# Two attention layers, chunk by chunk: a new order of the work, and the residual by way of DRAM

## The chip, the core and the metric

The kernel runs on one core of one Trainium2 chip. A core has a matrix engine (PE), a vector engine (DVE), an activation engine (ACT), a general-purpose engine (POOL) and a queue processor (SP) that here issues nearly all DMAs. Each engine carries out its own list of instructions strictly in the order in which it was written, and waits at an instruction until the semaphores that it needs are set. The metric is the device time of one execution in microseconds; the median of three executions is compared.

## What is computed

x is 2048 tokens by 512 numbers in float32. Four layers follow one another, A, B, A, B, each with a residual; both A layers share one set of weights and both B layers another.

```python
def _A_ref(x, wqkv, wo):            # 32 heads of 16, each query sees 8 keys: itself and back in steps of 2
    idx = pos[:, None] - off[None, :]          # off = 0, 2, ..., 14
    logits = jnp.einsum("bhsd,bhswd->bhsw", q, kg) * scale
    attn = _softmax(logits, axis=-1)
    o = jnp.einsum("bhsw,bhswd->bhsd", attn, vg)
    ... @ wo
def _B_ref(x, wqkv, wo):            # 32 heads of 16, each query sees the last 256 keys
    scores = jnp.einsum("bhqd,bhkd->bhqk", q, k) * (Dh ** -0.5)
    p = _softmax(scores, axis=-1)   # behind the causal window of 256
    ... @ wo
x = A_x
x = x + _A_ref(_layernorm(x, axis=-1), A_wqkv, A_wo)
x = x + _B_ref(_layernorm(x, axis=-1), B_wqkv, B_wo)
x = x + _A_ref(_layernorm(x, axis=-1), A_wqkv, A_wo)
x = x + _B_ref(_layernorm(x, axis=-1), B_wqkv, B_wo)
```

## The kernel before

**Tiling.** The tokens are cut into 8 chunks of 256. The loop at the end runs over the first pair of layers (A, B) for chunks 0 to 7, and then over the second pair: 16 chunk passes of layer A followed by layer B. Since A looks back 14 tokens and B 256, chunk c needs only chunk c and c - 1 of the layer before.

**One chunk in layer A** (`layer_a`): x is loaded into a tile `x` (L867). `norm` takes means and variances (L740 on DVE), one power on POOL (L744 to L747), normalizes on ACT (L759), transposes on PE (`pt`, L763) and splits the result into a high and a low float16 part (`xh` on ACT, `xl` on DVE). `proj_t` makes q, k and v on PE with three float16 products for each (`pq`, L788 to L790); ACT takes them out of PSUM. The logits are products of k and q, element by element, in 16 pieces of 128 x 512 (`pr`, L917), which PE sums over each head (`L`, L925). A softmax over 8 follows (DVE and ACT, L948 to L962), PE spreads the weights (`pb`, L984), DVE multiplies them with v in 8 pieces (`pw`, L997), and POOL (three additions, L1004 to L1006) or DVE (one reduction, L1002) sums each into `o`. `finish` splits `o` (`oh` on ACT, L827; `ol`, L829), multiplies with wo on PE (`po`, L807 to L809) and adds the result to x (L835 on DVE).

**One chunk in layer B** (`layer_b`): the same `norm` and projections. q and k go to DRAM and come back as stacked tiles `stk` (`re`, L1038, L1049). For each of 4 groups of heads PE makes scores `sq` (L1092, L1095), and DVE masks them and takes their row maxima (L1111, L1113; 32 such pairs a chunk). The maxima are turned on PE (`pm`), put beside the queries by a small DMA (`mt`, L1136), and PE makes the scores again, transposed and with the maximum taken off (`sk`, L1165, L1167). ACT takes the exponential (`p`, L1171), POOL zeroes what lies outside the window (L1180), and PE multiplies with v (`av`, L1197). `sq` and `sk` share two PSUM buffers (`q_sc`), so that PE can be at most two such scores ahead of DVE and ACT. The sums are gathered and divided by way of DRAM (`rc`, `scr`, `os`, `oc`, L1248 to L1271), and `finish` ends the layer.

**What sets the order.** Every piece of work is a task of a `Plan`, added with its engine, what it reads and writes, and a rough duration. A table `ORDER`, written as numbers, gives for each chunk and layer the place of each task in its engine's list; a negative number moves a task to its other engine, where it has one (`alt`: L917, L829, L962 and L1271 stand with DVE, L1002 and L1004 to L1006 are the two forms of one task). `Plan.order` merges the lists so that each task's buffers are free. The keys of the table are the preparation of A's weights and of B's (`pA`, `pB`), 110 groups of three matmuls on a constant that fill PE where it has nothing else (`W`, `idle`, L1309), and then `A0`, `B0`, ... `A15`, `B15`.

**Tile x.** The pool `px` has three buffers. A chunk's x stays in one of them from its load (L867) through A's residual (L835), B's norm and B's residual up to its store to DRAM (`xd`, L846, for the second pair; `out`, L840, at the end).

## Time and profile before

| | |
|---|---|
| median of 3 executions | 1500.89 us (1498.52 to 1501.27) |
| the profiled execution | 1504.43 us, its span 1502.7 us |
| busy: PE, DVE, ACT, POOL | 1374.5, 1210.1, 748.3, 691.6 us |
| granted clock of PE, mean | 0.977 |
| products `pr` (L917) on DVE, on POOL | 225, 31 |
| sums of `pw` on POOL (L1004 to L1006), on DVE (L1002) | 100, 28 |
| moved by DMA | 96.33 MB in 73090 packets |

Busy times are of one profiled execution and of the engine's own work, without waits. PE's busy time is that of matmuls that overlap one another, with modelled ends. The rows of "waits" name an instruction, what it waited for, the time in total, how often, and the longest. In the chain of waits each piece is followed back to what released it.

### The profile page before, as it was taken

The numbers are of one execution on the slowest core, as the hardware profiler recorded it, in microseconds if no ns is written. First come the engines' busy times: TensorE is split into PE (matmuls) and PEld (weight loads), VectorE is DVE, ScalarE is ACT, GpSimd is POOL, SyncE is SP. The second block draws the span as 40 slices with busy tenths as digits, with TensorE's granted clock in tenths as the row PEclk, the third lists the DMA queues.
The fourth block names the chain that finished last, engine by engine and source line by source line (L and its number), as shares of the span: only waits on it lengthen the run. The fifth ranks groups of instructions, "written<-read, shape, count | busy, mean of one in ns | idle before, by whom it ended". The sixth has DMA issues, their size and how long they took to land.

```text
span 1502.7 us, 35144 instructions
## 1 busy us (share of the span) xinstructions
PE 1374.5 (91%) x14186; PEld 797.5 (53%) x14186; DVE 1210.1 (81%) x2153; ACT 748.3 (50%) x1075; POOL 691.6 (46%) x854
## 2 busy tenths in 40 slices
PE   6888989989899998989999898998989899998988
PEld 4464645647365463745546363654636465463544
DVE  5958797887968878796987968798797978889674
ACT  6431444554555555555544444555554555455554
POOL 2414254373734638273462527345372645637232
PEclk9999999999999999999989998999999999999999
DMA  7021112222121221212122222112212121222221
GB/s 251 16 55 52 49 43 62 70 54 86 33 79 46 62 78 40 93 33 81 41 59 79 52 88 52 63 50 68 72 45 87 33 79 53 68 70 47 69 62 43
DMA packets 73090, 96.33 MB, mean 64 GB/s; under 512 B 17120, under 2 KB 44256, under 8 KB 72928
## 3 DMA queue, kind: packets, MB, share of 16 engines
q1 hardware_dynamic: 72672, 93.83, 22.1%
q8 instruction: 111, 1.82, 0.5%
q14 instruction: 51, 0.42, 0.1%
q10 hardware_dynamic: 256, 0.26, 0.1%
HBM read 49.81 MB, written 34.05 MB: 56 GB/s over the span
## 4 chain that ended last, share of the span: by engine, by line
PE 57%; DVE 15%; POOL 10%; DMA 6%; issue 5%; ACT 4%; SPq 3%; DVEq 0%; ACTq 0%; POOLq 0%
PE pq L788 8%; PE pq L789 7%; PE pq L790 7%; PE av L1197 6%; PE sk L1165 4%; PE L L925 4%; DVE m L1113 3%; PE po L807 3%; PE sq L1092 3%; DVE pw L997 3%; POOL pw L1004 3%; PE po L809 3%; PE po L808 3%; ACT p L1171 2%; DVE sq L1111 2%
## 5 line engine op out<-in xcount | busy, mean ns | idle before, releaser
L1171 ACT ACTIVATE p<-sk,sclB 128x768 f32<-128x768 f32 x480 | 425.0, 899 | 301.9 <-PE sk L1167 254.6
L1180 POOL TENSOR_SCALAR_AFFINE_SELECT p<-p 128x1024 f32<-128x1024 f32 x240 | 263.8, 1107 | 437.6 <-ACT p L1171 429.7
L1113 DVE TENSOR_REDUCE m<-sq 128x2 f32<-128x512 f32 x448 | 310.4, 693 | 15.4
L1111 DVE COPY_PREDICATED sq<-maskt,sq 128x256 f32<-128x256 int16 x448 | 188.7, 421 | 91.6 <-PE sq L1095 85.3
L1197 PE MATMUL av<-p,v 128*32 128x128 f32 (+1 forms) x3840 | 200.1, 332 | 6.9 <-POOL p L1180 6.5
L917 DVE TENSOR_TENSOR pr<-kv,q 128x512 f32<-128x512 f32 x225 | 158.8, 762 | 32.7 <-PE L L925 11.8
L1165 PE MATMUL sk<-stk,stk 64*128 64x256 f16 x960 | 133.9, 280 | 34.6 <-ACT p L1171 16.6
L1197 PEld LDWEIGHTS av<-p,v 128*32 128x32 f32 x3840 | 104.8, 109 | 99.2 <-issue 34.6
L997 DVE TENSOR_TENSOR pw<-pb,kv 128x1024 f32<-128x1024 f32 x128 | 152.8, 1213 | 4.4 <-PE pb L984 2.8
L1092 PE MATMUL sq<-stk,stk 48*128 48x128 f16 (+1 forms) x896 | 114.3, 252 | 33.0 <-ACT p L1171 15.8
L1004 POOL TENSOR_TENSOR pw<-pw 128x512 f32<-128x512 f32 x100 | 127.0, 1270 | 34.8 <-DVE pw L997 34.6
L1095 PE MATMUL sq<-stk,stk 48*128 48x128 f16 (+1 forms) x1024 | 126.8, 246 | 6.7 <-DVE m L1106 3.8
L1165 PEld LDWEIGHTS <-stk 64*128 64x128 f16 x960 | 54.6, 94 | 137.8 <-issue 95.8
L1092 PEld LDWEIGHTS <-stk 48*128 48x128 f16 x896 | 49.2, 94 | 126.1 <-issue 83.9
L1167 PE MATMUL sk<-stk,stk 64*128 64x128 f16 x960 | 107.1, 219 | 0.0
L917 POOL TENSOR_TENSOR pr<-kv,q 128x512 f32<-128x512 f32 x31 | 41.5, 1345 | 101.9 <-PE L L925 72.6
L759 ACT ACTIVATE xn<-x,rs 128x512 f32<-128x512 f32 x64 | 51.9, 810 | 63.3 <-POOL rs L747 57.8
L1005 POOL TENSOR_TENSOR pw<-pw 128x256 f32<-128x256 f32 x100 | 72.7, 727 | 7.8
L788 PE MATMUL pq<-xh,wA0h 128*128 128x256 f16 x256 | 71.3, 279 | 2.2 <-DVE el L1028 2.2
L1028 DVE SCALAR_TENSOR_TENSOR el<-pq,eh 128x512 f16<-128x512 f32 x64 | 43.5, 686 | 35.9 <-ACT eh L1025 24.2
L788 PE MATMUL pq<-xh,wA2h 128*128 128x256 f16 x256 | 70.5, 275 | 0.8 <-DVE pscA L691 0.8
L789 PE MATMUL pq<-xl,wA0h 128*128 128x256 f16 x256 | 70.9, 277 | 0.2 <-DVE xl L769 0.2
(181 smaller groups left out, 3176.1 us busy)
## 6 DMA issues: line engine op xcount, KB each, us to landing
stk<-re SPq DMA_DIRECT2D x256, 96.0 KB
re<-eh SPq DMA_DIRECT2D x128, 128.0 KB
re<-el SPq DMA_DIRECT2D x64, 128.0 KB
oc<-os SPq DMA_DIRECT2D x120, 64.0 KB
os<-scr SPq DMA_DIRECT2D x15, 512.0 KB
x<-in_A_x_dram SPq DMA_DIRECT2D x8, 512.0 KB
xd<-x SPq DMA_DIRECT2D x16, 256.0 KB
x<-xd SPq DMA_DIRECT2D x8, 512.0 KB
```

The lines of the kernel that those rows point to most:

```text
L788: nc.tensor.matmul(ps[mp].t[:, i], wh, xh, start=k == 0, stop=False)
L789: nc.tensor.matmul(ps[mp].t[:, i], wh, xl, start=False, stop=False)
L917: E.tensor_mul(pr.t, window(kv[1].t, m, 64 * tq, 64)[:, 0], qb)
L997: nc.vector.tensor_mul(pw.t, pb.t.unsqueeze(1).broadcast_to([P, 2, W, 64]), v)
L1004: E.tensor_add(t[:, :, 0:4], t[:, :, 0:4], t[:, :, 4:8])
L1092: nc.tensor.matmul(ps.t[:, par, 0 : (2 - qb) * P], lhs, stk[hf, bef][r, col, qb * P :], start=True, stop=True)
L1111: nc.vector.copy_predicated(t[:, :, 0:P], maskt[:, 0:P].bitcast(I16).unsqueeze(1).broadcast_to([P, 2, P]), t[:, :, 2 * P : 3 * P])
L1113: nc.vector.tensor_reduce(out=m.t[:, qb, :, u], in_=t[:, :, 0 : 2 * P], op=ALU.max, axis=AX.X)
L1165: nc.tensor.matmul(o[:, two], k[:, jf * P : (jf + 1) * P], q, start=True, stop=True)
L1171: nc.scalar.activation(pt.t[:, :, 2 * i : 2 * i + 2].rearrange("p s m q -> p m s q"), ps.t[:, :, : 3 * P].rearrange("p m (s q) -> p m s q" ...
L1180: nc.gpsimd.affine_select(out=v, in_=v, pattern=[[0, 8], [-1 if b == 0 else 1, P]], compare_op=ALU.is_gt if b == 0 else ALU.is_ge, fill=0. ...
L1197: nc.tensor.matmul(o, v[:, jj, 17 * h : 17 * h + 32], rhs, start=z == 0 and (b == 0 or first), stop=z == 1 and b == 1, tile_position=(0, 3 ...
```

## The change

x no longer stays in its tile from A to the end of B. After A's residual each half of it is also stored to a DRAM tile `xm` (L849 of the new kernel), and `finish` of layer B loads it again into a new tile `xr` of the same pool (L828), adds to that, and stores from there. So the tile of A is free once B's norm has read it and the stores have landed. The constants of the planner, the pools and all arithmetic stay as they are.

```diff
         T = layers[l]
         xb, vx = x_in[c]
+        if T == "B":
+            mid, vmid = x_mid[c]
+            xb = buf("px", [P, 2, D], F32, "x", f"xr{l}_{c}")
+            vx = [Val(xb), Val(xb)]
+            plan.add("SP", 0.5, lambda: nc.sync.dma_start(xb.t, mid.t.rearrange("(t p) d -> p t d", p=P)), r=vmid, w=vx, size=512)
...
-            plan.add("DVE", 0.67, done, r=[vps, vscl[T, 3]], w=[vx[t]])
-            if T == "B":
+            plan.add("DVE", 0.67, done, r=[vps, vscl[T, 3], vx[t]], w=[vx[t]])
+            if T == "A":
+                if t == 0:
+                    mid = buf("dram", [C, D], F32, "xm", f"xm{l}_{c}")
+                    x_mid[c] = mid, [Val(mid), Val(mid)]
+                plan.add("SP", 0.4, lambda t=t, mid=x_mid[c][0]: nc.sync.dma_start(
+                    mid.t[t * P : (t + 1) * P], xb.t[:, t]), r=[vx[t]], w=[x_mid[c][1][t]], size=256)
+            else:
```

All numbers of `ORDER` are new. Its rows tell a reader nothing by themselves; one line of each stands for the table:

```diff
     "A9": [
-        307, 706, 707, 281, 541, 1362, 543, 712, 544, 1366, 545, 714, 266, 282, 1374, 1375, 1378, 1380, 1384, 1387, 1388, 1396, 551, 555, 1379, 1381,
+        273, 578, 602, 303, 485, 1325, 511, 623, 512, 1330, 515, 625, 301, 347, 1345, 1346, 1354, 1358, 1340, 1350, 1351, 1359, 526, 528, 1337, 1338,
```

What the table moves is seen in the engines' lists. In a name such as `pr_5_0_3` the 5 is the chunk, and the last number is a running one.

**DVE, the logits' products of chunk 5** (first pair of layers), while the row maxima of layer B's chunks 3 and 4 (L1111, L1113) are taken. Before:

```order
L1113 TENSOR_REDUCE m_3_3_5533<-sq_3_3_2_0_5719 128x2
L917 TENSOR_TENSOR pr_5_0_3_5773<-kv_5_1_5547,q_5_5765 128x512
L917 TENSOR_TENSOR pr_5_0_1_5784<-kv_5_1_5547,q_5_5765 128x512
L917 TENSOR_TENSOR pr_5_0_0_5791<-kv_5_1_5547,q_5_5765 128x512
L917 TENSOR_TENSOR pr_5_0_2_5806<-kv_5_1_5547,q_5_5765 128x512
L1111 COPY_PREDICATED sq_3_3_2_1_5793<-maskt,sq_3_3_2_1_5793 128x2x128
L1113 TENSOR_REDUCE m_3_3_5533<-sq_3_3_2_1_5793 128x2
L917 TENSOR_TENSOR pr_5_1_2_5834<-kv_5_1_5547,q_5_5765 128x512
```

Now (L930 is the old L917, L1124 and L1126 the old L1111 and L1113):

```order
L930 TENSOR_TENSOR pr_5_0_2_5715<-kv_5_1_5085,q_5_5484 128x512
L1124 COPY_PREDICATED sq_3_3_1_1_5717<-maskt,sq_3_3_1_1_5717 128x2x128
L1126 TENSOR_REDUCE m_3_3_5624<-sq_3_3_1_1_5717 128x2
L842 SCALAR_TENSOR_TENSOR xr_2_5480<-po_2_1_5667,sclB_185,xr_2_5480 128x512
L771 SCALAR_TENSOR_TENSOR xl_4_5757<-pt_4_1_5727,xh_4_5738 128x4x128
L930 TENSOR_TENSOR pr_5_0_0_5761<-kv_5_1_5085,q_5_5484 128x512
L1124 COPY_PREDICATED sq_3_3_0_0_5742<-maskt,sq_3_3_0_0_5742 128x2x128
L1126 TENSOR_REDUCE m_3_3_5624<-sq_3_3_0_0_5742 128x2
```

Chunk 5 had 14 of its 16 products on DVE, in runs of three and four within 21 rows; now 10 are there, the first two of them one at a time between row maxima.

**POOL, the other products of chunk 5** among the masks (L1180, now L1193) of layer B's chunk 3, whose `p` PE waits for. Before there were two, one behind the other; now:

```order
L930 TENSOR_TENSOR pr_5_0_3_5687<-kv_5_1_5085,q_5_5484 128x512
L1193 AFFINE_SELECT p_3_1_1_5639<-p_3_1_1_5639 128x1024
L930 TENSOR_TENSOR pr_5_1_3_5794<-kv_5_1_5085,q_5_5484 128x512
L930 TENSOR_TENSOR pr_5_1_1_5819<-kv_5_1_5085,q_5_5484 128x512
L1193 AFFINE_SELECT p_3_2_0_5759<-p_3_2_0_5759 128x1024
L930 TENSOR_TENSOR pr_5_1_0_5866<-kv_5_1_5085,q_5_5484 128x512
L930 TENSOR_TENSOR pr_5_1_2_5885<-kv_5_1_5085,q_5_5484 128x512
L1193 AFFINE_SELECT p_3_2_1_5706<-p_3_2_1_5706 128x1024
```

Of the 240 masks, 20 stood directly behind a product in POOL's list; now 42 do. Over the whole program, with the number of instructions before and now: products on DVE 225 and 140, on POOL 31 and 116; reductions L1002 on DVE 28 and 21, and their three-addition forms on POOL 100 and 107; the rest of the softmax weights (L962) on DVE 9 and 1, on POOL 7 and 15; the division's product (L1271) on DVE 17 and 6, on POOL 13 and 24; the low part `ol` (L829) on DVE 19 and 12, on POOL 45 and 52. Nothing else changes its engine.

**SP, the way of x.** Before, a load of x stood behind the store of the chunk three passes earlier, in whose buffer it goes (chunk 2's store and chunk 5's load):

```order
L1049 DMA stk_2_122<-re_3_1_4300 48x1x1024 x2
L1263 DMA os_2_1_4878<-scr_2_5157 128x1x1024
L1136 DMA stk_0_117<-mt_3_1_5255 2x4x256 x2
L846 DMA xd_5370<-x_2_200 128x512 x2
L867 DMA x_5_5423<-in_A_x_dram 128x2x512
L1049 DMA stk_0_120<-re_3_0_4416 48x1x1024 x2
L1038 DMA re_4_1_5537<-eh_4_1_5515 64x2x512
```

Now, in the same part of the program (L1149 is the old L1136, L1051 the old L1038):

```order
L828 DMA xr_2_5480<-xm_2_3487 128x2x512
L849 DMA xm_4_5578<-x_4_3452 128x512
L1149 DMA stk_0_117<-mt_3_1_5626 2x4x256 x2
L849 DMA xm_4_5578<-x_4_3452 128x512
L880 DMA x_6_5763<-in_A_x_dram 128x2x512
L1149 DMA stk_0_120<-mt_3_2_5918 2x4x256 x2
L1051 DMA re_4_1_5953<-eh_4_1_5874 64x2x512 x2
L859 DMA xd_5968<-xr_2_5480 128x512
```

The load of chunk 6 now stands behind A's residual of chunk 4 and ahead of the store of chunk 2's result; before, it stood behind the store of chunk 3's. On PE, layer A's projections of chunk 6 now begin when 12 of the 32 scores `sq` of layer B's chunk 4 stand ahead of them; before, 28 did.

**Both ends of PE's list.** Before, one group of `idle` stood ahead of the transposes (L763) of the first chunk's second half and none ahead of the first's; 68 of the 110 groups stood ahead of chunk 1's projections in layer B, and 42 later, 16 of these right ahead of the last `po`. Now all 110 stand in the first chunks, some 60 of them, with the preparation of all of A's and most of B's weights, ahead of the first transposes; the projections of chunk 1 in layer A stand ahead of those of chunk 0 in layer B, and nothing fills PE before the last `po`.

More of the change, by code (lines that the diff above doesn't have):

```diff
@@ L724 @@
     x_in = {}
+    x_mid = {}
     st8 = {}
```

8 lines of the change are left out of this document (4 added, 4 removed), and 491 rows, old and new, of the table ORDER.

## The prediction

> **What bounds the kernel now.** I read the page first, then the busy times by stretches, the waits of each engine, the chain of waits near one reload of x, and the groups by line with shapes kept apart. The page:
>
> ```profile
> span 1502.7 us, 35144 instructions
> PE 1374.5 (91%) x14186; PEld 797.5 (53%) x14186; DVE 1210.1 (81%) x2153; ACT 748.3 (50%) x1075; POOL 691.6 (46%) x854
> PE 57%; DVE 15%; POOL 10%; DMA 6%; issue 5%; ACT 4%; SPq 3%; DVEq 0%; ACTq 0%; POOLq 0%
> ```
>
> PE is busy for 91% of the span, yet only 57% of the chain that ended last is PE's work: for the rest PE's next matmul hung on somebody else. DVE comes next in both. The busy times by stretches (head, second part of the head, all of the steady part, tail; busy us with instructions behind, then clock and DMA) tell where PE is idle:
>
> ```profile
> 0.00:100.00 100.00, 73.43 (x490) 49.25 (x491) 69.90 (x135) 51.37 (x78) 30.02 (x62) 0.93 0.30 102
> 100.00:300.00 200.00, 183.35 (x1744) 110.32 (x1742) 162.04 (x344) 80.26 (x120) 74.15 (x96) 0.97 0.23 61
> 300.00:1444.00 1144.00, 1067.77 (x11366) 612.38 (x11365) 946.08 (x1620) 585.68 (x840) 566.25 (x678) 0.98 0.23 62
> 1444.00:1503.00 59.00, 49.94 (x593) 25.52 (x589) 32.09 (x57) 31.01 (x39) 21.19 (x19) 1.00 0.17 47
> ```
>
> The columns of busy time are PE, PEld, DVE, ACT, POOL. PE is idle for 26.6 + 16.7 us in the head, 76.2 in the steady part (1144 - 1067.8) and 9.1 in the tail, 128 us in all. In the steady part DVE is busy for 946.1 of 1144 us, 83%: too much to be always there when a score lands. The waits say so:
>
> ```profile
> PE sk L1165 <- ACT p L1171: 16.6, 34, 1.1
> PE sq L1092 <- DVE m L1113: 14.9, 33, 1.4
> PE sk L1165 <- DVE m L1113: 14.1, 30, 1.4
> PEld L1092 <- DVE m L1113: 30.7, 59, 1.7
> PEld L1165 <- DVE m L1113: 30.1, 56, 1.7
> PE av L1197 <- POOL p L1180: 6.5, 12, 1.5
> PEld av L1197 <- POOL p L1180: 17.2, 36, 1.7
> POOL p L1180 <- ACT p L1171: 429.7, 120, 11.6
> ```
>
> Whichever score PE makes next, it waits for DVE to empty one of the two score buffers: 29.0 us of waiting matmuls and 60.8 us of waiting weight loads, many small pieces of at most 1.7 us. For POOL's masks the same sum is 23.7 us. A third tie is x itself. Here is the chain across one chunk boundary (start, us, what):
>
> ```profile
> 1219.24 4.01 DMA out_dram<-x
> 1223.31 4.05 DMA x<-xd
> 1227.38 0.70 DVE b L740
> ```
>
> The new chunk's first instruction waits for a load of 4.05 us, and that for a store of 4.01 us out of the same buffer. So the kernel is bound by PE with about 7% of holes in the steady part, and the holes come from a busy DVE and from chunks that start no sooner than x's buffer is free.
>
> **The change, part by part.** First, work leaves DVE. The groups that have two forms:
>
> ```profile
> L917 DVE TENSOR_TENSOR pr<-kv,q 128x512 f32<-128x512 f32 x225 | 158.8, 762 | 32.7 <-PE L L925 11.8 <-ACT kv L898 11.6 <-ACT q L896 8.5
> L917 POOL TENSOR_TENSOR pr<-kv,q 128x512 f32<-128x512 f32 x31 | 41.5, 1345 | 101.9 <-PE L L925 72.6 <-ACT kv L898 15.3 <-ACT q L896 9.8
> L1002 DVE TENSOR_REDUCE o<-pw 128x128 f32<-128x1024 f32 x28 | 53.9, 1930 | 0.5
> L1271 DVE TENSOR_TENSOR oc<-oc,os 128x512 f32<-128x512 f32 x17 | 13.9, 840 | 3.8 <-DMA os<-scr 3.7
> L962 DVE TENSOR_TENSOR e<-e,eh 128x512 f16<-128x512 f32 x9 | 6.3, 695 | 0.1
> L829 DVE TENSOR_TENSOR ol<-oc,oh 128x512 f16<-128x512 f32 x10 | 7.4, 750 | 5.1 <-ACT oh L827 5.1
> L1004 POOL TENSOR_TENSOR pw<-pw 128x512 f32<-128x512 f32 x100 | 127.0, 1270 | 34.8 <-DVE pw L997 34.6
> L1005 POOL TENSOR_TENSOR pw<-pw 128x256 f32<-128x256 f32 x100 | 72.7, 727 | 7.8
> L1006 POOL TENSOR_TENSOR o<-pw 128x128 f32<-128x128 f32 x100 | 45.9, 459 | 7.8
> ```
>
> The counts of the order give what goes: 85 products by 0.762 = 64.8 us, 7 reductions by 1.930 = 13.5, 11 divisions' products by 0.840 = 9.2, 8 rests of the weights by 0.695 = 5.6, 7 low parts by 0.750 = 5.2, together 98 us. DVE falls to about 1112 us, 74% of today's span. POOL gains 85 x 1.345 = 114 us, 7 x (1.270 + 0.727 + 0.459) = 17, and 26 of the other pieces at, by estimate, about 1.3 each (they are as large as a product) = 34: some 165, to 856 us, 57%. So both have room.
>
> What that is worth lies between nothing and the 76.2 us of holes in the steady part. I take three quarters, **-57 us**: DVE is what the scores wait for most, it becomes 8% lighter, its row maxima no longer stand behind runs of three and four products (2.3 to 3.0 us by the row above, in which no score buffer comes free), and the reload of x joins the same holes. That last part alone is 13 loads, each standing behind a store, at up to 8.1 us a piece on the chain: at most 105, but most chunk starts are prepared well ahead, and DVE's own wait says how little is left:
>
> ```profile
> DVE b L740 <- DMA x<-in_A_x_dram: 6.6, 3, 4.7
> DVE b L740 <- DMA x<-xd: 6.4, 4, 2.3
> ```
>
> 13.0 us in all. The greater gain of the free buffer is that PE has projections of a chunk further ahead to put between scores, and these wait for nobody. I count it in the three quarters.
>
> With fewer holes the clock falls less often. The mean granted clock, 0.977 on the query of cores, withholds 2.3% of the span, 35 us at most. I take a quarter of it, **-9** (bounds 0 and -20).
>
> ```profile
> core 0: 1502.7 us, clock 0.977
> ```
>
> POOL's masks come later. 22 more of them stand right behind a product, at
>
> ```profile
> L917 POOL TENSOR_TENSOR pr<-kv,q x31: 1169/1187/1686, 184.5 to 1340.6; 128x512 f32<-128x512 f32 x31
> ```
>
> a median of 1.187 us: 26 us more if PE felt all of it, nothing if none. `av` is queued behind the mask, all later PE work behind `av`. PE now feels 23.7 us over 240 masks; POOL waits for ACT before half of the masks, 430 us in all by the row above, and a product can fit in that wait. **+10**.
>
> x by way of DRAM: 32 stores and 16 loads more on SP.
>
> ```profile
> L846 SPq DMA_DIRECT2D xd<-x x16: 320/325/432, 245.7 to 869.8; - x16
> L867 SPq DMA_DIRECT2D x<-xd x8: 371/377/378, 696.1 to 1311.0; - x8
> 785.99 2.00 DMA xd<-x
> 788.01 5.37 DMA x<-xd
> ```
>
> Issuing takes 32 x 0.325 + 16 x 0.377 = 16 us of SP over the run, one microsecond a chunk. The store waits for DVE's residual and holds back the `stk` and `mt` transfers queued behind it, for which PE's scores wait; the load needs 5.4 us, and the order has it far ahead of B's residual, so that it is hidden by the division and by `po`. If that cover were gone, 16 x 5.4 = 86 us. I take **+3** (0 to +20).
>
> The tail: the fillers ahead of the last `po` go.
>
> ```profile
> 1486.83 5.41 PE L1309 MATMUL idle<-selt 128*128 128x256 f16 x48
> 1493.21 0.39 PE L807 MATMUL po<-wB3h,oh 128*128 128x512 f16 x1 [0.97 <-ACT oh L827]
> ```
>
> PE will be idle there for some 6 us, and if the clock drops, the last 24 matmuls from 1493.2 to about 1498.9 take twice their 5.7 us. **+4** of 0 to +6. The Trainium skill's "TensorE: Matmul & The Clock Gate", section "What's actually happening", has the clock halve after an idle window of about 3.4 us; by it the 6 us suffice, and the term would be +6 at the least favourable phase.
>
> The head: A's first transposes now stand behind the preparation of nearly all weights, B's too. They begin at
>
> ```profile
> 10.79 1.12 PE L763 MATMUL pt<-idf,xn 128*128 128x128 f32 x4 [1.84 <-ACT xn L759]
> ```
>
> and will begin up to 20 us later, since 60 fillers of three matmuls stand ahead of them (by the row of 48 in 5.41 us, 180 take 20 us); in return B's first chunk no longer waits for its weights, and chunk 1's projections are done ahead of it, while PE idles 43 us of the first 300. I take **0** (-15 to +15).
>
> Sum: -57 - 9 + 10 + 3 + 4 + 0 = -49 us. The profiled execution took 1504.4 us (span 1502.7 and 1.7 around it), so 1455; it stood 3.5 us above the median shown, so **1452 us**.
>
> **The rivals.** *The port between DVE and POOL* ends on the other side. The product on DVE shows what happens when POOL reads at the same time:
>
> ```profile
> L917 DVE TENSOR_TENSOR pr<-kv,q x225: 669/684/1720, 29.2 to 1346.1; 128x512 f32<-128x512 f32 x113
> ```
>
> Most take 0.684 us, the mean is 0.762, the worst 1.720. With POOL busy for 57% and products on both engines at once, each of the 140 that stay could take 1.04 us more: 146 us, less 98 saved and less the 11 of such delay that these 140 hold today, is +37 us of DVE work, and the masks' +26 stand beside it. PE's holes would grow as DVE's load grows: I put half of the 37 and half of the 26 on the end, +31, **1532 us**. It decides from about 94 hit products on (94 x 1.04 = 98). For it: twice as many POOL instructions read SBUF while chunks' products run. Against it: products of one chunk stand on DVE in rows where POOL has masks to wait for, and today's mean is only 78 ns above the median. The Trainium skill's "SBUF — State Buffer", section "SBUF: two separate sides", says that the pair of ports is an exclusive lock, and that the loser of a DVE instruction with two SBUF inputs and a reading GpSimd instruction is blocked for the whole of the other; the 1.720 agrees with that.
>
> *PE is the limit as it stands*: its 1067.8 busy us of the steady part contain everything, and the holes only move to other places. Then the -57 and the +10 fall away; the clock's -9, the transfers' +3 and the tail's +4 remain, with up to 15 of the head either way: -2, **1499 us**. For it: PE 91%. Against it: PE's busy time contains matmuls that run slowly in a half clock or alone.
>
> *All holes go*: -76, -20 of clock, -15 in the head, +10 for POOL and tail: **1400 us**. For it: DVE at 74% and PE with work in reserve. Against it: ACT, too, releases scores, and `sk` waits for it as long as for DVE.
>
> **How the numbers follow.** The forecast (1425 to 1482) has a chance of 0.44, all holes gone (1380 to 1425) 0.16, PE as the limit (1482 to 1512) 0.20, the port (above 1512, some of it less) 0.20. Leaving out a third of the second and most of the last gives the range **1402 to 1512**; the forecast's own is 1425 to 1482. About 0.2%, 3 us, is what a measurement can tell from no change. Faster: 0.44 + 0.16 + half of 0.20 = 0.70; the same 0.05; slower 0.25.
>
> **What would show it.** In the new profile PE's idle time in the steady part should fall from 76 us toward 20, DVE's busy time be near 1112 us and POOL's near 856, PE's waits for L1113's successor shrink from 90 us to under 60, the new chunk's L740 wait for no load, the granted clock rise above 0.98. Products on DVE with a mean near 0.78 us speak against the port, near 1.2 for it. A first transpose later than 25 us with a layer B no later than now confirms the head. Wrong would be: `av` waiting more than 50 us for masks, B's residual waiting for `xr`, or PE's holes as many as now with DVE at 74%: then DVE was not what made them.

## The result, and the profile after

The changed kernel takes 1446.85 us (1444.62 to 1448.24) against 1500.91 us before: a ratio of 0.9642, with an interval from 0.9625 to 0.9658. The forecast was 1452 us. The profiled execution took 1447.4 us, its span is 1445.7 us, 57.0 us shorter than the one before. The page of the new kernel:

```profile
span 1445.7 us, 35284 instructions
PE 1350.3 (93%) x14186; PEld 791.4 (55%) x14186; DVE 1127.4 (78%) x2035; ACT 743.9 (51%) x1075; POOL 837.5 (58%) x986
```

DVE is 83 us lighter and POOL 146 us heavier, so the work went where the diff sends it. PE is the surprise: the same 14186 matmuls are busy for 24.2 us less. The span's 57.0 us are thus 32.8 us of PE's idle time and 24.2 us of its busy time.

Where along the program? Here are the busy times by stretches, first of the kernel before, then of the new one. I cut where the transposes of layer B's norm begin for chunk pass 3 and for pass 15, which are the same instructions in both kernels: head, twelve whole periods, tail. The columns are PE, PEld, DVE, ACT, POOL, then clock and DMA.

```profile
0.00:332.70 332.70, 285.39 (x2512) 172.06 (x2512) 262.04 (x521) 147.37 (x220) 130.94 (x190) 0.96 0.25 72
332.70:1389.00 1056.30, 989.00 (x10491) 572.67 (x10490) 877.25 (x1505) 540.84 (x777) 525.97 (x633) 0.98 0.23 62
1389.00:1502.70 113.70, 100.10 (x1184) 52.75 (x1184) 70.82 (x129) 60.11 (x79) 34.70 (x32) 1.00 0.20 58
```

```profile
0.00:328.60 328.60, 301.70 (x2768) 191.64 (x2768) 255.93 (x511) 151.04 (x227) 166.99 (x225) 0.98 0.28 84
328.60:1325.30 996.70, 955.14 (x10379) 555.43 (x10375) 804.43 (x1404) 532.46 (x770) 638.12 (x732) 0.99 0.27 77
1325.30:1445.70 120.40, 93.48 (x1045) 44.37 (x1045) 67.08 (x121) 60.39 (x80) 32.38 (x30) 0.87 0.24 72
```

All of the gain lies in the twelve periods: 1056.3 to 996.7 us, or 88.0 to 83.1 us a period. The head gives 4.1 us more, and the tail takes 6.7 us back. In the middle PE's idle time falls from 67.3 to 41.6 us (-25.7), its busy time by 33.9 us. One source of the second number is the clock. The twelve windows of one period each (the first and the last of them, before and then after):

```profile
332.70:423.90 91.20, 84.22 (x902) 47.75 (x901) 72.53 (x117) 46.03 (x67) 51.15 (x58) 0.98 0.21 58
1303.10:1389.00 85.90, 81.86 (x894) 48.27 (x892) 75.31 (x122) 45.87 (x66) 43.99 (x52) 1.00 0.24 65
```

```profile
328.60:413.10 84.50, 83.14 (x917) 48.76 (x913) 69.20 (x114) 46.84 (x68) 54.27 (x64) 1.00 0.27 77
1244.20:1325.30 81.10, 72.80 (x801) 37.11 (x799) 64.66 (x107) 41.54 (x59) 51.18 (x55) 0.98 0.24 68
```

Each row's length times what its clock lacks of 1.00, summed over the twelve, is 21 us before and 5 us now: 16 of the 33.9. Some 10 us more are work that moved and wasn't saved: of the projections `pq`, 2760 matmuls lie in this stretch where 2880 lay before (340.5 us in place of 350.2), and the head has 120 more. The remaining 8 us the trace doesn't separate.

The waits of PE in the new kernel (L1105 is the old L1092, L1178 the old L1165):

```profile
PE sq L1105 <- DMA stk<-re: 17.7, 23, 1.9
PE sq L1105 <- DVE m L1126: 12.6, 28, 1.0
PE sk L1178 <- ACT p L1184: 8.2, 13, 1.5
PE sk L1178 <- DVE m L1126: 7.7, 18, 1.3
PE sq L1105 <- ACT p L1184: 3.6, 8, 1.0
PE av L1210 <- POOL p L1193: 1.9, 6, 0.9
PEld L1105 <- DVE m L1126: 32.6, 65, 1.4
PEld L1178 <- DVE m L1126: 30.7, 72, 1.5
```

A score waits for one of its two buffers, which DVE or ACT sets free. Matmuls stood for these two 61.4 us before (the 16.6, 14.9 and 14.1 that the prediction shows, and 15.8 of `sq` for ACT); now it is 32.1. More of that came off ACT's part (32.4 to 11.8) than off DVE's (29.0 to 20.3), though ACT has the same work as before. The weight loads' waits for DVE, 60.8 us then, are 63.3 now. And a new wait heads the list: 17.7 us for `stk`, the stacked tiles that come back from DRAM.

### The profile page after: what moved, and what is told of

Same layout as the page of the kernel before. It is cut to its first block, busy times and chain, and to the rows that moved or that the text cites. A ratio compares the mean times of both kernels' runs of the same rounds, so it can differ in the third digit from the quotient of the medians.

```text
span 1445.7 us, 35284 instructions
## 1 busy us (share of the span) xinstructions
PE 1350.3 (93%) x14186; PEld 791.4 (55%) x14186; DVE 1127.4 (78%) x2035; ACT 743.9 (51%) x1075; POOL 837.5 (58%) x986
## 5 line engine op out<-in xcount | busy, mean ns | idle before, releaser
L1193 POOL TENSOR_SCALAR_AFFINE_SELECT p<-p 128x1024 f32<-128x1024 f32 x240 | 264.2, 1108 | 314.5 <-ACT p L1184 302.3
L1126 DVE TENSOR_REDUCE m<-sq 128x2 f32<-128x512 f32 x448 | 310.4, 693 | 15.5
L1124 DVE COPY_PREDICATED sq<-maskt,sq 128x256 f32<-128x256 int16 x448 | 189.3, 423 | 104.2 <-PE sq L1108 98.3
L930 POOL TENSOR_TENSOR pr<-kv,q 128x512 f32<-128x512 f32 x116 | 138.8, 1211 | 59.9 <-PE L L938 58.0
L1010 DVE TENSOR_TENSOR pw<-pb,kv 128x1024 f32<-128x1024 f32 x128 | 154.2, 1216 | 11.7 <-POOL o L1019 6.0
L1178 PE MATMUL sk<-stk,stk 64*128 64x256 f16 x960 | 129.9, 278 | 21.3 <-ACT p L1184 8.2
L1017 POOL TENSOR_TENSOR pw<-pw 128x512 f32<-128x512 f32 x107 | 136.2, 1273 | 23.1 <-DVE pw L1010 23.0
L1105 PE MATMUL sq<-stk,stk 48*128 48x256 f16 (+1 forms) x896 | 114.9, 253 | 34.9 <-DMA stk<-re 17.7
L1108 PE MATMUL sq<-stk,stk 48*128 48x256 f16 (+1 forms) x1024 | 125.0, 248 | 4.8 <-DVE m L1119 2.0
L1105 PEld LDWEIGHTS <-stk 48*128 48x128 f16 x896 | 48.2, 94 | 129.9 <-issue 57.6
L1178 PEld LDWEIGHTS <-stk 64*128 64x128 f16 x960 | 50.9, 93 | 117.8 <-issue 73.7
L930 DVE TENSOR_TENSOR pr<-kv,q 128x512 f32<-128x512 f32 x140 | 98.3, 743 | 10.0 <-ACT q L909 5.3
L1180 PE MATMUL sk<-stk,stk 64*128 64x128 f16 x960 | 104.0, 217 | 0.0
L1018 POOL TENSOR_TENSOR pw<-pw 128x256 f32<-128x256 f32 x107 | 78.0, 729 | 8.4
L938 PE MATMUL L<-pr,sel 128*32 128x512 f32 x512 | 70.1, 601 | 2.8 <-DVE pr L930 1.7
```

The costliest lines, as they stand in the source:

```text
L930: E.tensor_mul(pr.t, window(kv[1].t, m, 64 * tq, 64)[:, 0], qb)
L1010: nc.vector.tensor_mul(pw.t, pb.t.unsqueeze(1).broadcast_to([P, 2, W, 64]), v)
L1017: E.tensor_add(t[:, :, 0:4], t[:, :, 0:4], t[:, :, 4:8])
L1105: nc.tensor.matmul(ps.t[:, par, 0 : (2 - qb) * P], lhs, stk[hf, bef][r, col, qb * P :], start=True, stop=True)
L1108: nc.tensor.matmul(ps.t[:, par, (2 - qb) * P : 3 * P], lhs, stk[hf, now][r, col, : (1 + qb) * P], start=True, stop=True)
L1124: nc.vector.copy_predicated(t[:, :, 0:P], maskt[:, 0:P].bitcast(I16).unsqueeze(1).broadcast_to([P, 2, P]), t[:, :, 2 * P : 3 * P])
```

## The experiments

Theory 1, the prediction's: DVE is what the scores wait for, and a lighter DVE makes the gain. Theory 2: the order makes it, because PE now has another chunk's projections between scores for most of a period. Beside these, each end of the list, POOL and the way of x have a term of their own to be priced.

### A lighter DVE in the old order

```diff
-                    E.tensor_mul(pr.t, window(kv[1].t, m, 64 * tq, 64)[:, 0], qb)
+                    if tq in LIGHT.get((l, c), {}).get(m, ()):      # 160 of DVE's 225 products
+                        E.tensor_mul(pr.t[:, 0:1], window(kv[1].t, m, 64 * tq, 64)[:, 0][:, 0:1], qb[:, 0:1])
+                    else:
+                        E.tensor_mul(pr.t, window(kv[1].t, m, 64 * tq, 64)[:, 0], qb)
...
```

> The old kernel, in which 160 of DVE's 225 products compute 64 of their 512 columns only (part of layer A's logits is then another product's): some 96 us less work on DVE, as much as the change takes from it, with the old order and nothing added to POOL. Theory 1 (the lighter DVE makes the gain): 1445 to 1470, with PE's waits for the row maxima under 60 us. Theory 2 (the order makes it): 1480 to 1500, with DVE idle for longer and PE's holes nearly as before.

Measured: 1497.9 us, ratio 0.9978 (0.9962 to 0.9993). DVE falls by 75.0 us, less than the 96 that I had put down, since a short product still takes 281 ns. These 75 us, nine tenths of what the change takes from DVE, are worth 3 us. The page, and its waits:

```profile
PE 1378.1 (92%) x14186; PEld 797.3 (53%) x14186; DVE 1135.1 (76%) x2153; ACT 749.1 (50%) x1075; POOL 686.9 (46%) x854
PE sk L1186 <- ACT p L1192: 15.9, 32, 1.1
PE sq L1113 <- DVE m L1134: 14.6, 31, 1.7
PE sk L1186 <- DVE m L1134: 14.4, 30, 1.4
PE sq L1113 <- ACT p L1192: 12.3, 22, 1.2
```

With DVE at 76% the matmuls wait for the row maxima exactly as long as with DVE at 81% (29.0 us both times). Theory 1 falls as the prediction has it: 1497.9 us is not 1445 to 1470. But the products might simply have been taken from the wrong place, so I looked where in a period the holes are. In the old order a chunk's projections of A (`pq`) are over at 60% of the period. From there to 90% PE has scores, `av` and the small matmuls of A's attention only. Busy times of the kernel before in that stretch of the twelve periods (the first, the last, and the sum):

```profile
387.40:414.80 27.40, 22.67 (x216) 8.86 (x214) 23.75 (x35) 13.15 (x18) 22.87 (x27) 0.94 0.22 54
1354.70:1380.40 25.70, 23.08 (x254) 9.80 (x248) 25.29 (x35) 13.75 (x20) 21.20 (x25) 1.00 0.20 43
sum 316.80, PE 263.55 PEld 109.08 DVE 295.09 ACT 155.94 POOL 270.02; mean PE 21.96 PEld 9.09 DVE 24.59 ACT 12.99 POOL 22.50
```

53.3 of the middle's 67.3 us of idle PE lie in this 30% of it, where DVE is 93% busy. The shortened products had run earlier, between 30 and 50% of the period, where PE has projections. In the run with them, the same stretch still has DVE 92% busy and PE idle for 49.9 us:

```profile
sum 317.40, PE 267.53 PEld 109.20 DVE 291.77 ACT 153.10 POOL 268.41; mean PE 22.29 PEld 9.10 DVE 24.31 ACT 12.76 POOL 22.37
```

### A lighter DVE in the right place

The next run takes as much from DVE (76 us by its page), 49 us of it inside this stretch: the products `pw` of weights and v run there for the most part.

```diff
-                    nc.vector.tensor_mul(pw.t, pb.t.unsqueeze(1).broadcast_to([P, 2, W, 64]), v)
+                    # k = 1 for five of a chunk's eight pieces, else W
+                    nc.vector.tensor_mul(pw.t[:, :, 0:k], pb.t[:, 0:k].unsqueeze(1).broadcast_to([P, 2, k, 64]), v[:, :, 0:k])
...
```

> The old kernel, in which 5 of the 8 products of weights and v of each chunk (pw, on DVE) compute one of their eight keys only, and the sums behind them run at full size on what is there (layer A's output is then another): 80 pieces by an estimated 0.9 us = some 72 us less work on DVE, about the 75 us that the run with shortened logits' products took from it (1210.1 to 1135.1). There the time fell by 0.2% only. In the old trace the logits' products stand where PE has projections and DVE is 76 to 90% busy; the pw stand in the part of each period in which PE has no projection, DVE is 95 to 97% busy, and PE is idle for 4.4 of the 5.6 us that it is idle per period. Theory of the place (what counts is DVE's load in that part): the time falls by 25 us or more, to 1475 or below, and PE's waits for row maxima by a third. Rival (two score buffers: each score waits for the latency of mask and maximum, whatever else DVE does): 1490 to 1502, waits as before.

Measured: 1486.41 us, ratio 0.9893 (0.9874 to 0.9913). So the place counts, five times as much as with the products, but it is 15 us and not the 25 or more of the theory of the place; the time lies between that theory's range and its rival's. The same stretch in this run, and then in the changed kernel:

```profile
sum 313.80, PE 267.49 PEld 110.83 DVE 246.31 ACT 159.84 POOL 259.59; mean PE 22.29 PEld 9.24 DVE 20.53 ACT 13.32 POOL 21.63
```

```profile
sum 299.10, PE 291.79 PEld 184.99 DVE 262.26 ACT 132.50 POOL 256.46; mean PE 24.32 PEld 15.42 DVE 21.85 ACT 11.04 POOL 21.37
```

This pair speaks for theory 2. With DVE only 78% busy the old order still leaves PE idle for 46.3 us; the new order, with DVE 88% busy, for 7.3 us. What differs most in this stretch is PE's own list: now projections of the next chunk run through this stretch (`pq` is busy there for 143 us in place of next to nothing), and their matmuls hardly wait for anybody, 2.8 us in the whole new trace. PE's matmuls waited for DVE and ACT for 57.0 us in the run with the short `pw`, 61.4 before, 32.1 in the new order. The new kernel holds a check of its own: in its twelfth period no further chunk is left to project, and there the same stretch has its holes again, 4.4 us, as many as a period of the old kernel on the mean, against 2.9 us in the other eleven together:

```profile
1292.80:1317.20 24.40, 20.03 (x220) 8.53 (x218) 23.12 (x36) 12.09 (x17) 21.87 (x26) 1.00 0.36 82
```

So with two score buffers and too little to put between, PE waits for the time that one score needs through mask, maximum or exponential, even where DVE has a fifth of its time left. No run moved the projections alone, though, so what the order gives without the lighter DVE stays open.

Not all holes of the stretch are saved. They shrink by 46 us, but the twelve periods lose only 25.7 us of idle time: 20 us came back elsewhere. The tenth from 40 to 50% of a period has now next to no projections (8.8 of its 99.7 us; 49.3 of 105.5 before), and PE is idle there for 18.0 us in place of 1.3, of which 15.1 us are waits for `stk`.

### More work on DVE in the new order

```diff
-                    E.tensor_mul(pr.t, window(kv[1].t, m, 64 * tq, 64)[:, 0], qb)
+                    for _ in range(2 if E is nc.vector else 1):
+                        E.tensor_mul(pr.t, window(kv[1].t, m, 64 * tq, 64)[:, 0], qb)
```

> The new kernel, in which each of the 140 logits' products on DVE is made twice, one behind the other: 140 x 0.743 = 104 us more work on DVE, which comes to about 1231 us, 21 us above the old kernel's 1210. The order and all other work stay. Theory 1 (the gain comes from the lighter DVE): the waits of PE for the row maxima go back to 90 us or more, and most of the gain goes, to 1490 or above. Theory 2 (the gain comes from the new order, in which PE has work of another chunk at hand while DVE is late): it rises by less than a third of the 104 us, to 1450 to 1480.

Measured: 1525.0 us (1514.47 to 1529.91), ratio to the kernel before 1.0151 (1.0109 to 1.0193): 78 us of the 116 that DVE gained (1243.3 us busy). By the number this is theory 1's line, and theory 2's 1450 to 1480 fails; but the mechanism is not theory 1's. The profiled execution is the fastest, 1514.47 us:

```profile
PE L L938 <- DVE pr L930: 46.3, 36, 5.7
PE sq L1105 <- DVE m L1126: 15.9, 35, 0.8
PE sk L1178 <- DVE m L1126: 11.0, 24, 1.3
```

The waits for row maxima grow by 6.6 us only (20.3 to 26.9). What comes up is `L`, the sums over the products themselves: 46.3 us, against 1.7 in the changed kernel. The new order has PE take a product soon after DVE makes it, and where one takes twice as long, PE stands in front of `L` with all its other work queued behind. So the new order gives its gain only with its products on time, and the moves to POOL may well belong to that; whether it would work with the old split between DVE and POOL no run shows, since these products were lengthened and not moved back.

### Less work on POOL

```diff
+                    if tq in LIGHT.get((l, c), {}).get(m, ()):      # 106 of POOL's 116 products, one key of eight
+                        E.tensor_mul(pr.t[:, 0:1], window(kv[1].t, m, 64 * tq, 64)[:, 0][:, 0:1], qb[:, 0:1])
...
```

> The new kernel, in which 106 of POOL's 116 products compute 64 of their 512 columns only (part of layer A's logits is then another product's): some 100 us less work on POOL. If the masks' lateness costs the +10 us of the prediction, the time falls by 5 to 10 us, to 1437 to 1442. If POOL's products fit into its waits for ACT's exponentials (302 us in the new trace), it stays at 1445 to 1448. If the two engines hold each other up, DVE's products fall from their mean of 743 ns toward 670, and its busy time by 10 us more.

Measured: 1450.64 us, ratio 0.9669 (0.9639 to 0.9698); the changed kernel had 0.9642. POOL is 94 us lighter (743.9 us) and nothing is gained. Products on POOL fit into its waits for ACT, and the masks' term is nothing.

### x by way of DRAM

The route alone, in the old order: the change's edit of `finish`, and the old table with 48 places more for it on SP (in each chunk the stores behind A's residual, the load of `xr` ahead of B's division).

```diff
     "A0": [
-        45, 6, 46, 7, 68, 49, 8, 47, -51, 74, 53, 10, 52, 11, 78, 55, -57, 58, -60, 38, 12, 89, 91, 92, 94, 66, 41, -64, 96, 97, 98, 99, 68,
+        45, 6, 46, 7, 68, 49, 8, 47, -51, 74, 53, 10, 52, 11, 78, 55, -57, 58, -60, 38, 12, 89, 91, 92, 94, 66, 18.4, 41, -64, 96, 97, 98, 99, 68, 18.5,
```

> The old order with x by way of DRAM: 32 stores and 16 loads more on SP, the same places for all else, and each load of a new chunk's x where it was. It prices the route alone. The prediction's +3 would give 1501 to 1506. If the route by itself makes the gain, since x's buffer is free earlier, it is faster by 10 us or more (under 1490). If its transfers hold back those for the stacked queries and the maxima, slower by 10 us or more (above 1511).

Measured: 1500.54 us, ratio 1.0004 (0.9991 to 1.0017). The route by itself neither gains nor costs anything in the old order.

In the new order it can't be taken out: the projections of chunk pass 6 stand ahead of the output projection of pass 3 there, and three buffers for x don't reach so far without it. So I made its transfers twice:

```diff
-                nc.sync.dma_start(mid.t[t * P : (t + 1) * P], xb.t[:, t])
+                for _ in range(2):
+                    nc.sync.dma_start(mid.t[t * P : (t + 1) * P], xb.t[:, t])
...
-            nc.sync.dma_start(xb.t, mid.t.rearrange("(t p) d -> p t d", p=P))
+            for _ in range(2):
+                nc.sync.dma_start(xb.t, mid.t.rearrange("(t p) d -> p t d", p=P))
```

> The new kernel with every transfer of the DRAM route made twice: 64 stores and 32 loads of x instead of 32 and 16. The second copy costs what the first does: 16 us of issue on SP, and 16.8 MB of traffic more. Theory that the route is nearly free (the prediction's +3): the time rises by 0 to 5 us (1447 to 1452). Rival, the route's transfers and issues are what delays the reloads of stacked queries (in the new trace PE's matmuls of L1105 wait 17.7 us and its weight loads 25.4 us for the transfer from re to stk, 1.1 us and 2.1 us in the old one): these waits grow toward double and the time rises by 15 us or more (above 1460).

Measured: 1529.23 us, ratio 1.0177 (1.015 to 1.0204), some 80 us more than the changed kernel by the two ratios, far more than the theory of a nearly free route gave. The edit did more than double the traffic: a second transfer into the same place waits for the first. SP's waits, and one of DVE's:

```profile
SPq L854 <- DMA xm<-x: 70.9, 32, 4.3
SPq L829 <- DMA xr<-xm: 58.3, 16, 5.5
DVE xr L845 <- DMA xr<-xm: 27.0, 7, 7.5
```

SP stands for 129 us in these two rows, which the changed kernel doesn't have, with every other transfer queued behind it, and B's residual waits 27.0 us for `xr` (0.7 in the changed kernel). PE's wait for `stk` rises to 25.5 us. To tell standing still from traffic, the second copies then went into tiles in DRAM of their own:

```diff
+                    again = pools["dram"][0].tile([P, D], F32, tag=f"xa{t}", name=f"xa{l}_{c}_{t}")
+                    nc.sync.dma_start(again, xb.t[:, t])
...
+                again = pools["dram"][0].tile([C, D], F32, tag="xc", name=f"xc{l}_{c}")
+                nc.sync.dma_start(again, mid.t)
```

> The new kernel with one more transfer behind each of the DRAM route's 32 stores and 16 loads, of the same size, but into tiles in DRAM of its own, so that no copy waits for another: the issue on SP (32 x 0.325 + 16 x 0.377 = 16 us) and the traffic (16.8 MB written) once more, without a wait. In the run with each transfer made twice into the same place the time rose by 82 us, and SP stood there 70.9 us before the second stores and 58.3 us before the second loads, each until the first had landed. If it was this standing still (a queue in order holds up the stacked queries and x behind it), this run stays at 1447 to 1455. If traffic and issue cost it, it rises by 30 us or more, to 1477 or above, and the waits of PE for stacked queries double.

Measured: 1456.55 us, ratio 0.9698 (0.9672 to 0.9724): some 8 us more than the changed kernel by the two ratios, a little above the 1455 expected of a pure standing still. So of the 80 us about a tenth is issue and traffic, and the rest comes with the waits for the first copy: SP standing in a queue that is carried out in order, and B's residual held until the second copy of `xr` is there. The two parts of the rest no run separates. The waits for the stacked tiles didn't grow with the traffic:

```profile
PE sq L1113 <- DMA stk<-re: 16.5, 22, 2.4
PE sk L1186 <- DMA stk<-mt: 7.3, 4, 5.2
```

16.5 us, against 17.7: twice the route's traffic doesn't lengthen the new wait for `stk`. With the lengthened products on DVE it was 3.3 us, so it is small where PE is late. What it costs stays open.

### The head

```diff
-IDLE = 110
+IDLE = 50        # the 60 groups that stand ahead of the first transposes are left out
```

> The new kernel without the 60 filler groups ahead of the first transposes (some 20 us of PE). The prediction had the head at 0, with those fillers as a price of up to 20 us. If they are a price, layer B of the first chunk starts up to 15 us earlier and the time falls by 5 to 15 us (1432 to 1442). If they only fill the time in which the weights' preparation and x's norm hold PE up anyway, the first projections begin no earlier and the time stays within 2 us of 1447. If they keep the clock up through the preparation of the weights, it gets slower, by up to 7 us for each stretch at half clock (1449 to 1460).

Measured: 1430.14 us (1426.26 to 1430.99), ratio to the kernel before 0.9523 (0.9505 to 0.9542): 17 us faster than the changed kernel. Its first transposes, and those of the changed kernel:

```profile
30.45 1.12 PE L762 MATMUL pt<-idf,xn 128*128 128x128 f32 x4 [0.33 <-ACT xn L758]
```

```profile
36.80 0.61 PE L765 MATMUL pt<-idf,xn 128*128 128x128 f32 x4
```

The fillers delayed them by 6.4 us, and the three stretches, cut at the same instructions as above, show where the rest is:

```profile
0.00:321.30 321.30, 281.04 (x2589) 175.37 (x2590) 255.81 (x511) 151.31 (x228) 167.10 (x225) 0.99 0.29 86
321.30:1312.30 991.00, 956.73 (x10378) 555.01 (x10377) 805.21 (x1405) 532.64 (x770) 637.82 (x731) 0.99 0.27 77
1312.30:1429.30 117.00, 90.89 (x1044) 43.39 (x1042) 66.70 (x121) 59.87 (x80) 32.38 (x30) 0.90 0.26 74
```

7.3 us in the head, 5.7 in the twelve periods, 3.4 in the tail. The first is explained by the rows above, the others are not: the lists of these parts are the same. Such a split is that of one execution; how far it can be trusted shows below.

Without any filler in the head (and with 46 in the tail, see below), and with the last 50 of the head left in:

```diff
-IDLE = 110
+IDLE = 46        # the first: none in the head, 46 in the tail
...
+IDLE = 96        # the second: the last 50 of the head, 46 in the tail
```

> The new kernel without any filler in the head, and with 46 groups in the last chunk's layer B (those of the tail experiment). Without the first 60 groups it had gone from 1447 to 1430, and with the 46 in the tail to 1444. If all fillers of the head are a price, a further 50 x 0.34 = 17 us of PE go, part of them from the path: 1415 to 1425. If the 50 that stand behind the first transposes only fill gaps, it stays at 1426 to 1431. If they keep the clock up, some stretches at half clock appear in the first 300 us and it is 1432 to 1440.

> The new kernel without the 60 filler groups ahead of the first transposes and with the 46 in the last chunk's layer B. If the two effects add up, 1430.1 - 2.9 = 1427 (1424 to 1430). If the tail's fillers do nothing here, 1430.

Measured: 1437.74 us (1434.69 to 1441.55), ratio 0.9571 (0.9549 to 0.9594), without any; 1430.54 us (1427.61 to 1434.03), ratio 0.9522 (0.9498 to 0.9545), with the 50. So these seem to be worth 7 us, and the clock is the reason that one would look for: without them it is 0.87 between 60 and 100 us, with them 1.00. The three stretches, first without them and then with them, don't bear that out:

```profile
0.00:325.40 325.40, 274.86 (x2437) 164.85 (x2437) 256.48 (x511) 150.82 (x227) 166.98 (x225) 0.96 0.28 85
325.40:1318.90 993.50, 957.37 (x10378) 554.94 (x10374) 804.56 (x1404) 532.05 (x770) 638.22 (x732) 0.99 0.27 77
1318.90:1436.40 117.50, 102.66 (x1183) 55.19 (x1183) 66.97 (x122) 60.16 (x80) 32.43 (x30) 0.99 0.25 74
```

```profile
0.00:324.90 324.90, 286.14 (x2588) 177.16 (x2588) 256.00 (x511) 151.24 (x227) 166.83 (x225) 0.98 0.29 85
324.90:1310.40 985.50, 951.00 (x10376) 553.47 (x10374) 803.50 (x1404) 532.31 (x770) 637.83 (x732) 1.00 0.28 78
1310.40:1428.80 118.40, 102.88 (x1183) 55.30 (x1183) 67.18 (x122) 60.18 (x80) 32.42 (x30) 0.98 0.25 73
```

The heads end within 0.5 us of one another, and the 8 us lie in the twelve periods, whose lists are the same again. But the second of these kernels and the one with the edit of the head alone have the same lists in head and periods, and they split 324.9 and 985.5 against 321.3 and 991.0 us. So a part can be off by 4 to 6 us between single executions. That the fillers are worth 7 us of the whole is measured; in which part, and by way of the clock or not, these profiles don't tell. The same holds for the twelve periods of all kernels that differ only in fillers (985.5, 991.0, 993.5 and 996.7 us so far); PE's wait for `stk` (12.6, 8.5, 14.7 and 17.7 us) doesn't follow their order.

### The tail

```diff
-IDLE = 110
+IDLE = 126       # 16 groups right ahead of the last po, as in the old order
```

> The new kernel with 16 filler groups (48 matmuls on a constant, 5.4 us of PE in the old trace) right ahead of the last output projection, where the old order had 16. In the new trace PE stands idle there for 6.23 us and the last 24 matmuls take 8.2 us, against 5.7 in the old one. If the missing fillers slow the end by way of the clock (tail theory), those 24 go back to 5.7 us and the time falls by 2.5 us, to about 1444. If the clock of the tail is set by the idle time of the whole last 70 us and not by this gap, nothing changes beyond 1 us (1446 to 1448). If the fillers themselves run at half clock and delay the projection, slower by up to 5 us.

Measured: 1444.1 us, ratio 0.9619 (0.9592 to 0.9647), 2.7 us below the changed kernel, with intervals that overlap. The trace shows the 2.5 us: the first and the last of the 24 matmuls of `po`, in the changed kernel and then with the fillers:

```profile
1433.75 0.61 PE L809 MATMUL po<-wB3h,oh 128*128 128x512 f16 x1 [6.23 <-ACT oh L834]
1441.52 0.38 PE L811 MATMUL po<-wB3h,ol 128*128 128x512 f16 x1
```

```profile
1431.56 0.39 PE L809 MATMUL po<-wB3h,oh 128*128 128x512 f16 x1 [0.86 <-ACT oh L834]
1436.88 0.38 PE L811 MATMUL po<-wB3h,ol 128*128 128x512 f16 x1
```

7.8 us from start to start without fillers and 5.3 with them, 0.61 us for the first matmul and 0.39. With 30 further groups between the scores of the last chunk:

```diff
-IDLE = 110
+IDLE = 156       # 16 groups as above, 30 in the gaps of the last chunk's sq, sk and av
```

> The new kernel with 46 filler groups in the last chunk's layer B: the 16 of the run above and 30 in the gaps between its scores, from about 1372 us on. In the new trace 32 us of the last 75 ran with the clock granted at half, against 3.4 us at most per stretch before. Tail theory: the clock stays up, the scores and output projections of the tail run at full speed, and the time falls by 5 to 10 us, to 1437 to 1441. Rival: the tail is a chain through ACT, DVE and DMA in which PE's speed counts little; then it falls by the 2.5 us of the run above at most, and fillers that stand in the way of a score cost up to 5 us (1444 to 1452).

Measured: 1443.89 us, ratio 0.9617 (0.9595 to 0.964): nothing beyond the 16. The kernel with the last 50 fillers of the head, shown above, has these 46 as well as the edit of the head, and is no faster than with the edit of the head alone (1430.54 and 1430.14 us). Its tail has the clock back at 0.98, from 0.87 and 0.90, and takes 118.4 us; without fillers there it took 120.4 and 117.0. So PE's speed counts little in the tail. The edit of the head alone is the simplest of the two fastest kernels: 0.9523 of the one before, and about 0.988 of the changed one.

## Why the prediction was right, and where it was not

The time was right to 5 us. Term by term the reasons did less well, so that the sum came out this near is in part luck.

**The holes, -57: about the size, for the wrong reason.** In the prediction's own stretch of the steady part PE's idle time went from 76.2 us to

```profile
300.00:1388.00 1088.00, 1035.57 (x11259) 599.65 (x11257) 870.56 (x1520) 580.53 (x837) 675.06 (x773) 0.99 0.27 78
```

52.4, not toward 20. The step that failed is "DVE is what the scores wait for most, it becomes 8% lighter": nearly that much lighter, the old order gains 3 us, or 15 where it counts. The middle nevertheless gave 59.6 us, 25.7 of them as holes and 33.9 as shorter busy time of PE, which the prediction had taken as given. Some 10 of the 59.6 are projections that moved into the head. The step that fits stands beside the failed one, in a sentence without a number: PE has projections of a chunk further ahead to put between scores, and these wait for nobody. That was the term, with the reservation that a DVE that is late with its products takes the gain away again.

It could have been seen. "DVE 83%" was a mean over a stretch with two kinds of parts; cut into tenths of a period, four fifths of the holes in the twelve periods lie where `pq` is absent. And the weight loads' 60.8 us of waiting were added to the matmuls' 29.0, though a load's wait lies beside matmuls that still run: in the new kernel it is 63.3 us, and the time is gone all the same.

**The clock, -9: right in sum.** The mean granted clock rose from 0.977 to

```profile
core 0: 1445.7 us, clock 0.981
```

so it withholds 27 us of the span in place of 35. But this is -16 in the periods, nearly all of it in the stretch where the projections were missing (20 of the 21 us before); some -7 in the head (4% of 333 us, 2% of 329); and +16 in the tail (13% of 120), where it costs next to nothing.

**POOL's masks, +10: wrong, it is nothing.** `av` waits 1.9 us for them as a matmul (6.5 before), and 94 us less of POOL don't shorten the time. The doubt named in the prediction, that a product can fit into POOL's waits for ACT, was the answer.

**x by DRAM, +3: within its bounds, as far as the runs show.** In the old order the route costs nothing; in the new one a further copy of its transfers costs 8 us, and the price of the first no run gives. B's residual waits for `xr` for 0.7 us, so the load is covered, and the new chunk's norm waits for x for under 2 us (13.0 before): both as predicted.

**The tail, +4: 6.7 us in the trace,** of which the missing fillers are 2.5. The Trainium skill's "TensorE: Matmul & The Clock Gate", section "What's actually happening", has the clock halve after an idle window of some 3.4 us; the granted clock of 0.50 from 1433.7 to 1438 us and the matmuls of 0.61 us (0.39 at full clock) behind 6.23 us of idle time agree. The other 4 us are not the clock's, since they stay when it is restored. Nor is more work left for the tail: apart from fillers it has 1045 matmuls, 1064 before, and 121 instructions on DVE, 129 before. Their cause stays open.

**The head, 0: it was -4, and hid a price.** The first transposes came at 36.8 us, later than 25 as said, but 26 us later than before and not 20 at most; layer B's norm of pass 3 came at 328.6 in place of 332.7. The prediction priced the 60 fillers at up to 20 us and then set the gain of the prepared weights against them. The runs separate the two: the fillers account for only 6.4 us of the 26. Without them the head is 8 to 11 us better than before (324.9 and 321.3 us in the two kernels that have the last 50 alone), and the whole run 17 us better than the changed kernel, more than the head explains.

**DVE 1112, POOL 856:** 1127.4 and 837.5. Products on POOL cost 1.211 us on the mean, not the 1.345 of the 31 in the old trace.

**The rivals.** The port between DVE and POOL:

```profile
L930 DVE TENSOR_TENSOR pr<-kv,q 128x512 f32<-128x512 f32 x140 | 98.3, 743 | 10.0 <-ACT q L909 5.3 <-PE L L938 4.5
L930 DVE TENSOR_TENSOR pr<-kv,q x140: 669/685/1670, 47.8 to 1273.2; 128x512 f32<-128x512 f32 x140
```

A mean of 743 ns over a median of 685: the mean even fell, by 19 ns, with nearly four times as many products on POOL, and with 106 of those cut short it is 724. *PE is the limit as it stands* fell with PE's busy time, which isn't a constant of the work; its remark that holes only move to other places is borne out for 20 of the 46 us. *All holes go* fell with the 52.4 us.

## What to carry to other kernels

Before work is taken from an engine that others wait for, cut the steady part into tenths of a period and see where the waiting engine is idle, and what it lacks there: here PE lacked work that needs no score buffer, and a lighter DVE couldn't give it that. Look again afterwards: 20 of the 46 us that were filled came back elsewhere in the period. Wait times of weight loads are not lost time of the matmuls beside them, and a sum of engine loads over a stage hides that its holes sit in one third of it. Fillers that keep the clock up are a delay where the first real work stands behind them, and a higher clock gained little in a tail in which the rest didn't wait for PE. A split by stretches of two single executions is not good for 5 us: hold two kernels with the same lists side by side first.

## What was not expected of the hardware

**A queue in order, and one wait in it.** 48 transfers that wait for their forerunner (2.2 us a store, 3.6 a load) cost some 80 us; 48 transfers of the same size that wait for nobody cost 8. In this kernel it is the waiting that has a price, on SP and for B's residual, not the traffic.

**Half a clock at a small price.** In the tail the granted clock was 0.87, and lifting it to 0.98 gained 2.5 us in the trace. Between 60 and 100 us it was 0.87 without fillers and 1.00 with them, and the head ended at 325.4 us without, at 324.9 and 321.3 with them: a price between nothing and 4 us.

**The same list, other times.** The same lists of twelve periods took 985.5 and 991.0 us behind a head with 50 groups of fillers, 993.5 without any and 996.7 with 110. With the same head they differ by 5.5 us, so only a part of this can be the fillers'. These four kernels as a whole repeat within 4 us of their medians. The cause is open.

**Who is slowed by POOL.** Of the 140 products on DVE, 106 had POOL at work for a tenth of their time or less and took 684 ns on the mean; the 34 that met more of POOL's work took 928. The 128 products `pw`, whose one input lies in PSUM, took 1216 ns whether POOL worked for nine tenths of their time or more (80 of them) or for one tenth or less (11). These means are worked out from the start and end of each record. The Trainium skill's "SBUF — State Buffer", section "SBUF: two separate sides", ties the shared port to DVE instructions with two SBUF inputs, and both groups agree with that. If the loser is blocked for the whole of the other's instruction, as the prediction cites it, an estimate of the worst from these rows is about 1.9 us (0.685 + 1.211); the worst here is 1.670.
